# One planned order for four engines over the first phase of an attention and mixture-of-experts kernel

## The chip, the core and the metric

The kernel runs on one core of one Trainium2 chip. The metric is the device time in microseconds, the median of the runs. The engines are TensorE (PE in the rows; its weight loads are PEld), VectorE (DVE), ScalarE (ACT), GpSimd (POOL) and SyncE (SP), which issues most transfers.

## What is computed

```python
# q, k, v: (4, 8, 576, 64); window 64, causal
scores = q @ k.T / 8, masked to the last 64 positions
attn   = softmax(scores);  x = (attn @ v) as 2304 tokens x 512
# first MoE layer (dense): w_in 512x2048, w_out 2048x512
h = x @ w_in;  x = (h * sigmoid(1.702 * h)) @ w_out
# second: 8 experts, w1 512x1024, w2 1024x512, one expert a token
logits = x @ w_gate;  e = argmax(logits);  gate = softmax(logits)[e]
out = gate * (relu(x @ w1[e]) @ w2[e])
```

`w_in` and `w_out` come as 64-bit floating-point numbers, all else as 32-bit ones.

## The kernel before

**Chunks.** The 2304 tokens are nine chunks of 256 (`c`). Attention of a chunk is done in four pairs of heads (`p`), each in nine parts, the tuple `ATT`: `scores` (TensorE), `maxima` (VectorE), `exps` (ScalarE), `normalise` (two small VectorE operations and a 128x512 product, L239, on VectorE for chunks 0 and 1 and on GpSimd after), `probs_t` (TensorE transposes), `probs_out` (ScalarE, L253), `attend` (TensorE, L262), `x_hi` (ScalarE) and `x_lo` (VectorE). Every matmul operand is split into a high and a low part, and each product is done as three matmuls (L156 to L158, L163 to L166).

**Steps.** The first MoE takes 16 steps a chunk (`m`): `up_mm` (12 matmuls of 256 columns), `tanh` (ScalarE, L387), `act` (VectorE, L391), `g_hi` (ScalarE, L398), `g_lo` (VectorE, L404), `down` (6 matmuls of 512 columns). A step has a slot number; `down` of step m stands two slots behind its `up_mm`. Chunks 0 and 1 are interleaved, while the 16 weight blocks are loaded and converted (`CONV`: six parts on ScalarE and VectorE). The results stay in 8 `whi` and 8 `wlo` tiles of the pool `wp`, which has 8 of each; expert weights take the same tiles later.

**Routing.** After a chunk: two copies `y_out` (one ScalarE, one VectorE), 16 gate products `logits` (VectorE, L448; on TensorE for the last chunk), `route_a` and `route_b` (some 18 small VectorE operations, an exponential, two small matmuls) and two indirect scatters by GpSimd into `xbuf`, rows grouped by expert.

**The experts.** They run in order of their counts, with row capacities 384, 352, ... 256. `pick_first` names the first expert in the middle of the last chunk, `load_expert` and `prep_expert` bring its weights (`ws`) and split them (L151 ScalarE; L152, half on GpSimd and half on VectorE). The first expert's 256 rows known by then pass through seven of its steps (`SPLIT`) while the last chunk is routed. Then `pick_order`, the remaining rows, and the experts one after another follow.

**What sets the order.** TensorE's order is written out by hand all along (`manual_schedule`). Up to slot 31 (`MEND`) ScalarE, VectorE and GpSimd too follow a list, made by `plan()`: a small simulation with a price per part (`MODEL`: engine, us, PSUM banks taken and given back), which starts, whenever an engine is free, the first part by slot whose named dependencies are done, at most `AHEAD` slots early. Behind slot 31 the parts stand at slots chosen by hand (`at_slot`), and the compiler orders the three engines by its own model of costs. SyncE's queue is ordered by the compiler throughout.

Of the kernel before, what the change touches and what calls it, by code (L numbers as in the profile page):

```python
# [28 lines left out]
E = 8  # L29
# [23 lines left out]
def tile_model(  # L53
# [115 lines left out]
    sched = defaultdict(list)  # L169
# [197 lines left out]
    def w_lo(m, i):  # L367
        hi, lo = dst_t[m][i]
        eng = nc.gpsimd if (m, i) in LO_POOL else nc.vector
        eng.tensor_tensor(out=lo, in0=st_t[m][:, i], in1=hi.bitcast(F32), op=ALU.subtract)  # L370
# [84 lines left out]
    def y_transpose(c, b):  # L455
        t = ps.tile([P, KD, P], F32, tag="ps", name="yt")
        for k in range(KD):
            nc.tensor.transpose(t[:, k, :], r_t[c, b][:, k * P : k * P + P], ident)
        for z, eng in enumerate((nc.scalar, nc.vector)):
            yT = gp.tile([P, CH], F32, tag="th", name="yT", bufs=2)  # L460
            src = t[:, 2 * z : 2 * z + 2, :].rearrange("p k t -> p (k t)")
            if z == 0:
                nc.scalar.activation(out=yT, in_=src, func=AF.Copy)
            else:
                nc.vector.tensor_copy(out=yT, in_=src)
            yT_t[b, z] = yT

    def logits_pe(c, b):
# [8 lines left out]
        if b == 1:  # L477
            lg = sm.tile([P, 2, E], F32, tag="lgs", name="lgs")
            nc.vector.tensor_copy(out=lg, in_=lp.rearrange("p (b e) -> p b e", b=2))
            r_t[c] = lg  # L480

    def route_a(c):
# [13 lines left out]
        )  # L496
        nc.vector.tensor_tensor(out=lg, in0=lg, in1=mxb, op=ALU.subtract)
        nc.scalar.activation(out=lg, in_=lg, func=AF.Exp)
        r_t[c] = (ohb, lg)

    def route_b(c):
        (ohb, ex), ys0, ys1 = r_t[c], r_t[c, 0], r_t[c, 1]
        shp = [P, 2, E]
        rk = ps.tile([P, 512], F32, tag="ps", name="rk")
        rv = rk[:, 0 : 2 * E].rearrange("p (b e) -> p b e", b=2)
        nc.vector.tensor_tensor(out=cum[:, 1, :], in0=cum[:, 0, :], in1=ohb[:, 0, :], op=ALU.add)
        nc.tensor.matmul(out=rv, lhsT=tri, rhs=ohb, start=True, stop=False)
        nc.tensor.matmul(out=rv, lhsT=ones, rhs=cum, start=False, stop=True)
        sl = sm.tile(shp, F32, tag="sl", name="sl")
# [15 lines left out]
        for b, ys in enumerate((ys0, ys1)):  # L525
# [19 lines left out]
    def count_keys():  # L545
        rk = ps.tile([P, 512], F32, tag="ps", name="cn")
        nc.tensor.matmul(out=rk[0:1, 0:E], lhsT=ones[:, 0:1], rhs=cum[:, 0, :], start=True, stop=True)
        cnt = sm.tile([1, E], F32, tag="cnt", name="cnt")
# [7 lines left out]
    def pick_first():  # L556
        cnt, key = count_keys()
# [8 lines left out]
    def pick_order():  # L566
        cnt, key = count_keys()
# [20 lines left out]
        return cnt, rank  # L588
# [5 lines left out]
    xp2 = {}  # L594

# [37 lines left out]

    def load_rows(e, which_blocks=None):
# [14 lines left out]
    def rows_t(e, b):  # L649
# [6 lines left out]
        xg, ti, ga, eh, el = ex_t[e]  # L656
        n = blocks(e)[b][1]
        t = ps.tile([P, KD, P], F32, tag="ps", name="et")
        for k in range(KD):
# [3 lines left out]
        hv = eh[:, :, b * P : b * P + n]  # L663
        nc.scalar.activation(out=hv, in_=t[:, :, 0:n], func=AF.Copy)  # L664
        nc.vector.tensor_tensor(  # L665
            out=el[:, :, b * P : b * P + n], in0=t[:, :, 0:n], in1=hv.bitcast(F32), op=ALU.subtract
        )
        nc.vector.tensor_copy(out=ti[0:n, b : b + 1], in_=xg[0:n, b, DM + 1 : ROW])
        nc.vector.tensor_copy(out=ga[0:n, b : b + 1], in_=xg[0:n, b, DM : DM + 1])

    def e_up(e, m, c0=0, c1=None, skip=0):
# [7 lines left out]
        for k in range(KD):  # L679
# [5 lines left out]
            )  # L685
        if "o" in xp2:
# [516 lines left out]
```

## Time and profile before

| | us |
|---|---|
| median of 3 runs | 754.58 (754.38 to 758.11) |
| the profiled execution's own time | 757.56 |
| its span, first to last instruction | 755.8 |
| busy: TensorE | 720.1 |
| busy: VectorE | 474.4 |
| busy: ScalarE | 366.1 |
| busy: GpSimd | 90.9 |

The span is what the trace covers; the own time holds 1.8 us more around it. A busy time is the union of the recorded instructions of an engine. A matmul's recorded end includes its latency, so a busy TensorE need not issue without gaps; its starts tell that.

### The profile page before, as it was taken

The numbers are of one execution on the slowest core, as the hardware profiler recorded it, in microseconds if no ns is written. First come the engines' busy times: TensorE is split into PE (matmuls) and PEld (weight loads), VectorE is DVE, ScalarE is ACT, GpSimd is POOL, SyncE is SP. The second block draws the span as 40 slices with busy tenths as digits, with TensorE's granted clock in tenths as the row PEclk, the third lists the DMA queues.
The fourth block names the chain that finished last, engine by engine and source line by source line (L and its number), as shares of the span: only waits on it lengthen the run. The fifth ranks groups of instructions, "written<-read, shape, count | busy, mean of one in ns | idle before, by whom it ended". The sixth has DMA issues, their size and how long they took to land. (4 is left out here: it accounts for less than half of the span.)

```text
span 755.8 us, 14418 instructions
## 1 busy us (share of the span) xinstructions
PE 720.1 (95%) x5356; PEld 632.8 (84%) x5357; DVE 474.4 (63%) x1451; ACT 366.1 (48%) x911; POOL 90.9 (12%) x97
## 2 busy tenths in 40 slices
PE   4779999999999999999999999988999999999996
PEld 3569888788988898898889889867788888898995
DVE  5999876956774754945936737464487453768511
ACT  6899664443445344344535433252266533546410
POOL 2000011111211012021011110142100201101111
PEclk9899999999999999999999999999999999999999
DMA  9992279120223022112211000341498726797100
GB/s 342 385 380 112 87 273 309 39 88 15 102 75 100 4 74 102 53 50 75 74 38 66 1 29 1 103 145 59 139 306 293 275 84 232 253 325 244 74 26 26
DMA packets 45370, 103.16 MB, mean 136 GB/s; under 512 B 3951, under 2 KB 12143, under 8 KB 45040
## 3 DMA queue, kind: packets, MB, share of 16 engines
q1 hardware_dynamic: 42304, 92.74, 35.9%
q0 software_dynamic: 2992, 9.46, 3.3%
q8 instruction: 43, 0.70, 0.4%
q14 instruction: 31, 0.25, 0.1%
HBM read 86.41 MB, written 16.03 MB: 136 GB/s over the span
## 5 line engine op out<-in xcount | busy, mean ns | idle before, releaser
L156 PE MATMUL h<-xh,whi 128*128 128x256 f32 x576 | 165.1, 287 | 0.0
L158 PE MATMUL h<-xh,wlo 128*128 128x256 f32 x576 | 163.2, 283 | 0.1
L157 PE MATMUL h<-xl,whi 128*128 128x256 f32 x576 | 162.9, 283 | 0.0
L163 PE MATMUL y<-whi,gh 128*128 128x512 f32 x288 | 118.9, 413 | 5.3 <-ACT gh L398 5.3
L391 DVE SCALAR_TENSOR_TENSOR th<-th,h 128x256 f32<-128x256 f32 x144 | 60.1, 417 | 100.2 <-ACT th L387 99.4
L387 ACT ACTIVATE th<-h 128x256 f32<-128x256 f32 x144 | 54.7, 381 | 134.0 <-PE h L158 128.8
L156 PEld LDWEIGHTS h<-xh,whi 128*128 128x128 f32 x576 | 110.1, 191 | 6.2 <-issue 0.5
L164 PE MATMUL y<-wlo,gh 128*128 128x512 f32 x288 | 114.3, 397 | 0.0
L157 PEld LDWEIGHTS h<-xl,whi 128*128 128x128 f32 x576 | 110.0, 191 | 4.7
L158 PEld LDWEIGHTS h<-xh,wlo 128*128 128x128 f32 x576 | 109.9, 191 | 0.5 <-DVE wlo L370 0.5
L152 DVE TENSOR_TENSOR wlo<-ws,whi 128x1024 fp32r<-128x1024 f32 (+1 forms) x64 | 77.7, 1222 | 34.1 <-ACT whi L151 33.7
L398 ACT ACTIVATE gh<-th 128x256 fp32r<-128x256 f32 x144 | 60.0, 416 | 66.0 <-DVE th L391 64.8
L448 DVE CUSTOM_DVE_ANT_0 junk<-ys,wg 128x512 bf16<-128x512 f32 x128 | 89.1, 696 | 2.9 <-DMA wg<-in_w_gateT 1.5
L166 PE MATMUL y<-whi,gl 128*128 128x512 f32 x288 | 90.3, 395 | 0.6 <-DVE gl L404 0.4
L151 ACT ACTIVATE whi<-ws 128x1024 fp32r<-128x1024 f32 (+1 forms) x72 | 68.0, 960 | 40.9 <-DMA ws<-in_w 30.6
L156 PE MATMUL eh_ps<-eh,whi 128*128 128x256 f32 (+3 forms) x284 | 85.4, 301 | 0.7 <-ACT eh L664 0.7
L157 PE MATMUL eh_ps<-el,whi 128*128 128x256 f32 (+3 forms) x284 | 83.6, 294 | 0.3 <-DVE el L665 0.3
L158 PE MATMUL eh_ps<-eh,wlo 128*128 128x256 f32 (+3 forms) x284 | 83.5, 294 | 0.0
L404 DVE TENSOR_TENSOR gl<-th,gh 128x256 fp32r<-128x256 f32 x144 | 61.5, 427 | 25.2 <-ACT gh L398 21.6
L163 PEld LDWEIGHTS y<-whi,gh 128*128 128x128 f32 x288 | 54.7, 190 | 16.2 <-ACT gh L398 8.4
L239 POOL TENSOR_TENSOR pr<-pr,su 128x512 f32<-128x512 f32 x28 | 31.1, 1112 | 296.6 <-DVE su L237 190.4
L166 PEld LDWEIGHTS y<-whi,gl 128*128 128x128 f32 x288 | 53.9, 189 | 14.9 <-DVE gl L404 2.8
(135 smaller groups left out, 1177.3 us busy)
## 6 DMA issues: line engine op xcount, KB each, us to landing
ws<-in_w SPq DMA_DIRECT2D x64, 512.0 KB, 5.1
qkv<-in_qkv SPq DMA_DIRECT2D x36, 672.0 KB, 5.0
st<-in_w_in SPq DMA_DIRECT2D x16, 512.0 KB, 10.1
st<-in_w_out SPq DMA_DIRECT2D x16, 512.0 KB, 11.0
xbuf<-zt SPq DMA_DIRECT2D x8, 771.0 KB, 10.1
xg<-xbuf SPq DMA_DIRECT2D x17, 257.0 KB, 5.4
raw<-in_w SPq DMA_DIRECT2D x8, 512.0 KB, 7.2
wg<-in_w_gateT SPq DMA_DIRECT2D x2, 1024.0 KB, 15.7
```

Source lines behind the costliest of these rows:

```text
L151: nc.scalar.activation(out=hi, in_=raw, func=AF.Copy)
L152: lo_eng.tensor_tensor(out=lo, in0=raw, in1=hi.bitcast(F32), op=ALU.subtract)
L156: nc.tensor.matmul(out=o, lhsT=a[0], rhs=b[0], start=first, stop=False)
L157: nc.tensor.matmul(out=o, lhsT=a[0], rhs=b[1], start=False, stop=False)
L158: nc.tensor.matmul(out=o, lhsT=a[1], rhs=b[0], start=False, stop=last)
L163: nc.tensor.matmul(out=o, lhsT=a[0][:, s], rhs=b[0], start=first, stop=False)
L164: nc.tensor.matmul(out=o, lhsT=a[0][:, s], rhs=b[1], start=False, stop=False)
L166: nc.tensor.matmul(out=o, lhsT=a[1][:, s], rhs=b[0], start=False, stop=last)
L391: nc.vector.scalar_tensor_tensor(out=th, in0=th, scalar=1.0, in1=h_t.pop((c, m)), op0=ALU.add, op1=ALU.mult)
L398: nc.scalar.activation(out=gh, in_=th, func=AF.Copy)
L404: nc.vector.tensor_tensor(out=gl, in0=th, in1=gh.bitcast(F32), op=ALU.subtract)
L448: nc.vector.tensor_tensor_reduce(out=junk, in0=ys[:, 0:DM], in1=wg_t[e // 4][:, e % 4, :], scale=1.0, scalar=0.0, op0=ALU.mult, op1=ALU.ad ...
```

## The change

`normalise` does its product on VectorE in every chunk. `y_out` becomes `y_act` and `y_dve`; only the last chunk's second copy stays on VectorE. Expert 0's splits become `e_hi` (ScalarE) and `e_lo` (VectorE), GpSimd's half included. From chunk 3 on `attend_pair` issues the attention of two pairs and the next two pairs' scores as one part. Routing, gate, row, expert load and expert step functions are cut into parts by engine and get prices in `MODEL`; `plan()` then orders the whole first phase, the last chunk's routing, the loads of expert 0 and its first seven steps in one list. The manual order of ScalarE, VectorE and GpSimd is kept from the first slot until two steps behind that list. `pick_first` stands ahead of the last chunk, after chunk 6 is routed. Left out below: the same cutting of `y_transpose`, `logits_pe`, `rows_t`, `e_up` and `count_keys`, and the named dependencies of the routing and expert parts.

```diff
@@ -235,8 +234,7 @@
         pr, mx, su = unit_t[c, p]
         nc.vector.tensor_scalar_add(su, su, 1e-9)
         nc.vector.reciprocal(out=su, in_=su)
-        eng = nc.vector if c < 2 else nc.gpsimd
-        eng.tensor_tensor(
+        nc.vector.tensor_tensor(
             out=pr, in0=pr, in1=su.unsqueeze(2).to_broadcast([P, 4, P]), op=ALU.mult
...
@@ -417,13 +414,13 @@
     r_t = {}
-    def y_out(c, b):
-        ys = yp.tile([P, ROW], F32, tag="ys", name="ys")
-        if b == 0:
-            nc.scalar.activation(out=ys[:, 0:DM], in_=y_t[c][b], func=AF.Copy, scale=0.5)
-        else:
-            nc.vector.tensor_scalar_mul(ys[:, 0:DM], y_t[c][b], 0.5)
-        r_t[c, b] = ys
+    def y_act(c, b):
+        ys = r_t[c, b] = yp.tile([P, ROW], F32, tag="ys", name="ys")
+        nc.scalar.activation(out=ys[:, 0:DM], in_=y_t[c][b], func=AF.Copy, scale=0.5)
+
+    def y_dve(c, b):
+        ys = r_t[c, b] = yp.tile([P, ROW], F32, tag="ys", name="ys")
...
+    def ranks(c):
+        ohb = r_t[c][0]
...
+    def scatter(c):
+        su32 = r_t[c]
+        for b in range(2):
+            ys = r_t[c, b]
...
+        nc.scalar.activation(out=ew_t[e, j][0][:, 2 * z + h], in_=st_t[e, i][:, h], func=AF.Copy)
+
+    def e_lo(e, i, h):
+        j, z = divmod(i, 2)
+        hi, lo = [t[:, 2 * z + h] for t in ew_t[e, j]]
+        nc.vector.tensor_tensor(out=lo, in0=st_t[e, i][:, h], in1=hi.bitcast(F32), op=ALU.subtract)
     def load_rows(e, which_blocks=None):
...
     SLOTS = slot[NCH - 1, NM - 1] + 1
+    LAST = SLOTS - NM
+    END = NCH - 1
     DD = 2
...
-    DB = (0, 0.01, 0.02, 1, 3, 3.01, 4, 4.01, 4.02)
+    DB = (0, 0.01, 0.02, 0.03, 3, 3.01, 4, 4.01, 4.02)
...
-    RG = {0: (1, 0.6), 1: (5, 0.55), 2: (2, 0.5), NCH - 2: (1, 0.2), None: (1.5, 0.45)}
-    RL = (1, 2, 1, 2, 2, 3)
+    RG = {0: (1, 0.6), 1: (3, 0.55), 2: (2, 0.5), NCH - 2: (1, 0.35), None: (2, 0.45)}
...
-        return slot[c - 1, 0] + 8 * (p // 2) - (2 if c == 3 else 3)
-
+        return slot[c - 1, 0] + 8 * (p // 2) - 3
+
+    def attend_pair(c, q):
+        for p in (2 * q, 2 * q + 1):
+            attend(c, p)
+        if (c, q) != (END, 1):
+            scores_pair(*((c, 1) if q == 0 else (c + 1, 0)))
+
+    def scores_pair(c, q):
+        for p in (2 * q, 2 * q + 1):
+            scores(c, p)
...
+    def swap_pools():
+        at_cm.__exit__(None, None, None)
+        pools.append(tc.tile_pool(name="p2g", bufs=2, reuse_waits="tile"))
+        xp2["g"] = pools[0].__enter__()
+
+    def clear_rows():
+        with tc.issue_after(last_w[0].ins):
+            init_xbuf(yp.tile([P, ROW], F32, tag="ys", name="zt"))
...
-        normalise: ("DVE", 1.2, 0, 0), probs_t: ("PE", 0.5, 1, 0), probs_out: ("ACT", 0.6, 0, 0),
+        normalise: ("DVE", 0.95, 0, 0), probs_t: ("PE", 0.5, 1, 0), probs_out: ("ACT", 0.55, 0, 0),
         attend: ("PE", 0.7, 0, 0), x_hi: ("ACT", 0.35, 0, 0), x_lo: ("DVE", 0.4, 0, 1),
+        attend_pair: ("PE", 2.3, 2, 0), scores_pair: ("PE", 1.1, 2, 0),
...
+        y_act: ("ACT", 0.55, 0, 1), y_dve: ("DVE", 0.65, 0, 1), logits: ("DVE", 0.75, 0, 0),
+        route_a: ("DVE", 1.4, 0, 0), gate_exp: ("ACT", 0.22, 0, 0), ranks: ("PE", 0.1, 1, 0),
+        route_b: ("DVE", 1.7, 0, 1), scatter: ("POOL", 2.4, 0, 0),
+        y_transpose: ("PE", 0.45, 1, 0), yT_act: ("ACT", 0.4, 0, 0), yT_dve: ("DVE", 0.4, 0, 1),
+        logits_pe: ("PE", 1.0, 0, 0), lg_out: ("DVE", 0.2, 0, 1),
+        count: ("PE", 0.1, 1, 0), pick_first: ("DVE", 1.3, 0, 1), pick_order: ("DVE", 1.7, 0, 1),
+        load_expert: ("SP", 1.8, 0, 0), e_hi: ("ACT", 0.6, 0, 0), e_lo: ("DVE", 0.7, 0, 0),
+        first_rows: ("SP", 1.2, 0, 0), last_rows: ("SP", 0.6, 0, 0),
+        rows_t: ("PE", 0.5, 1, 0), rows_hi: ("ACT", 0.55, 0, 0), rows_lo: ("DVE", 0.9, 0, 1),
+        e_up: ("PE", 1.45, 1, 0), e_act: ("ACT", 0.4, 0, 0), e_rest: ("DVE", 0.4, 0, 1),
+        e_down: ("PE", 1.4, 0, 0),
+        load_gate: ("SP", 6.0, 0, 0), clear_rows: ("POOL", 1.0, 0, 0), swap_pools: ("NONE", 0, 0, 0),
     }
+    LAND = {"SP": 2.0, scatter: 2.9, load_expert: 3.5}
...
     def part(s, fn, *a, after=()):
-
-        if s < MEND:
-            parts[fn, a] = (s, [x for x in after if x is not None])
-        else:
-            at_slot(s, fn, *a, rank=1 if fn in ATT else 5)
+        parts[fn, a] = (s, [x for x in after if x is not None])
...
-                take += 2 * (k[0] is down and k[1][1] == 0)
-                if eng != "SP" and parts[k][0] > parts[left[0]][0] + AHEAD:
+                take += 2 * (k[0] in (down, e_down) and k[1][1] == 0)
+                if k[0] is logits_pe:
+                    take = 1 - k[1][1]
+                if k[0] is maxima and k[1][0] >= PAIR:
+                    give *= k[1][1] % 2
+                if k[0] is attend_pair and k[1] == (END, 1):
+                    cost, take = 1.1, 0
+                far = parts[k][0] - parts[left[0]][0]
+                if far > 3 * AHEAD:
+                    break
...
                     held = held or banks < take
                     continue
                 free[eng] = t + cost
...
+    part(att_slot(PAIR, 0), scores_pair, PAIR, 0, after=[(load_pair, (PAIR, p)) for p in range(2)])
+    for c in range(PAIR, NCH):
+        for q in range(2):
+            n = (c, 1) if q == 0 else (c + 1, 0)
+            after = [(probs_out, (c, p)) for p in (2 * q, 2 * q + 1)]
+            after += [(load_pair, (n[0], p)) for p in (2 * n[1], 2 * n[1] + 1) if n[0] < NCH]
+            part(att_slot(c, 2 * q) + 8, attend_pair, c, q, after=after)
...
-    for k, (fn, a) in enumerate(plan()):
-        at_slot(BEGIN + (MEND - 0.5 - BEGIN) * k / len(parts), fn, *a)
+
+    part(slot[0, NM - 1], load_gate, after=[(load_w, (NM - 1,))])
+    part(slot[0, NM - 1] - 3, clear_rows, after=[(load_w, (NM - 1,))])
...
+        y = [(y_act, (c, 0)), (y_dve if c == END else y_act, (c, 1))]
+        for b, (fn, a) in enumerate(y):
+            part(s + 0.01 * b, fn, *a, after=[
+                (down, (c, NM - 1)), (scatter, (c - 2 + b,)) if c else (clear_rows, ()),
+            ])
...
+    part(LAST - 1, swap_pools, after=[(x_lo, (END, p)) for p in range(4)])
+    part(LAST - 0.9, count, 0, after=[(route_b, (NCH - 3,))])
+    part(LAST - 0.8, pick_first, after=[(count, (0,))])
+    part(LAST + 9, first_rows, after=[(scatter, (NCH - 2,)), (pick_first, ()), (swap_pools, ())])
...
+    EW, ED = 5, 1.2
+    for i in range(8):
+        p = LAST + EW + ED * i
+        part(p - 3, load_expert, 0, i, after=[
+            (pick_first, ()), (swap_pools, ()), *[(e_lo, (0, i - 2, h)) for h in range(2)]
+        ])
+        for h in range(2):
+            part(p + 1 + 0.4 * h, e_hi, 0, i, h, after=[(load_expert, (0, i))])
+            part(p + 1.1 + 0.4 * h, e_lo, 0, i, h, after=[(e_hi, (0, i, h))])
...
+    part(SLOTS + 2, last_rows, after=[(scatter, (END,))])
+    part(SLOTS + 3, count, 1, after=[(route_b, (END,))])
+    part(SLOTS + 3.1, pick_order, after=[(count, (1,))])
...
+        staged = tc.manual_schedule(
+            engines={mybir.EngineType.Activation, mybir.EngineType.DVE, mybir.EngineType.Pool}
+        )
+        staged.__enter__()
+        for fn, a in plan():
+            fn(*a)
...
-        rows = load_rows(0, blocks(0)[2:])
-        cnt, rank = pick_order()
...
+            if i == 2:
+                staged.__exit__(None, None, None)
```

## Rows read from the trace of the kernel before

**Rows 1.** The page, busy us (share of the span) xinstructions, per engine.
```profile
PE 720.1 (95%) x5356; PEld 632.8 (84%) x5357; DVE 474.4 (63%) x1451; ACT 366.1 (48%) x911; POOL 90.9 (12%) x97
```

**Rows 2.** Busy time by stretch: length, busy us (x) per engine, PEclk, DMA share, GB/s.
```profile
139.30:142.70 3.40, 3.40 (x22) 2.72 (x19) 3.37 (x11) 2.23 (x11) 1.37 (x1) 0.50 0.46 164
135.70:142.70 7.00, 5.22 (x35) 4.32 (x34) 6.72 (x32) 5.04 (x21) 1.37 (x1) 0.76 0.23 81
...
25.10:57.80 32.70, 25.74 (x230) 21.23 (x227) 31.39 (x75) 31.49 (x75) 0.00 (x0) 0.98 1.06 383
57.80:126.60 68.80, 68.80 (x521) 61.07 (x519) 53.80 (x128) 50.07 (x115) 3.66 (x5) 1.00 0.55 191
142.70:456.70 314.00, 313.78 (x2575) 279.14 (x2574) 192.36 (x761) 136.35 (x429) 40.33 (x37) 1.00 0.17 57
456.70:507.90 51.20, 48.17 (x300) 42.13 (x299) 32.99 (x100) 19.84 (x47) 9.03 (x8) 1.00 0.27 83
507.90:537.30 29.40, 25.78 (x164) 22.04 (x163) 11.78 (x41) 7.41 (x19) 5.72 (x6) 1.00 0.23 64
```

**Rows 3.** Timeline of PE in chunk 4: start us, us, instruction; [idle before <-releaser].
```profile
257.81 0.28 PE L156 MATMUL h<-xh,whi 128*128 128x256 f32 x1
...
260.62 0.28 PE L156 MATMUL h<-xh,whi 128*128 128x256 f32 x1
...
262.05 0.40 PE L163 MATMUL y<-whi,gh 128*128 128x512 f32 x1
...
263.53 0.69 PE L262 MATMUL t<-pr,qkv 128*64 128x64 f32 x16
264.14 0.39 PE L156 MATMUL h<-xh,whi 128*128 128x256 f32 x1
...
265.77 0.69 PE L262 MATMUL t<-pr,qkv 128*64 128x64 f32 x16
```

**Rows 4.** Timeline of PE at the end of chunk 2's attention.
```profile
139.09 0.97 PE L262 MATMUL t<-pr,qkv 128*64 128x64 f32 x16 [1.78 <-ACT pr L253]
```

**Rows 5.** Waits in the last chunk: us in total, times, longest us.
```profile
ACT whi L151 <- DMA ws<-in_w: 7.1, 5, 2.5
```

**Rows 6.** Timeline of PE in the passage.
```profile
507.96 0.28 PE L156 MATMUL eh_ps<-eh,whi 128*128 128x256 f32 x1
...
514.18 0.66 PE L458 MATMUL yt<-ident,ys 128*128 128x128 f32 x4 [0.84 <-ACT ys L423]
...
537.39 0.44 PE L156 MATMUL eh_ps<-eh,whi 128*128 128x384 f32 x1 [0.69 <-ACT eh L664]
```

**Rows 7.** Groups by line and shape: busy us, mean ns | idle before <-releasers.
```profile
L404 DVE TENSOR_TENSOR gl<-th,gh 128x256 fp32r<-128x256 f32 x144 | 61.5, 427 | 25.2 <-ACT gh L398 21.6 <-PE y L166 2.9
L391 DVE SCALAR_TENSOR_TENSOR th<-th,h 128x256 f32<-128x256 f32 x144 | 60.1, 417 | 100.2 <-ACT th L387 99.4
L398 ACT ACTIVATE gh<-th 128x256 fp32r<-128x256 f32 x144 | 60.0, 416 | 66.0 <-DVE th L391 64.8
...
L387 ACT ACTIVATE th<-h 128x256 f32<-128x256 f32 x144 | 54.7, 381 | 134.0 <-PE h L158 128.8 <-PE rk L508 3.7 <-PE cn L547 1.5
...
L239 POOL TENSOR_TENSOR pr<-pr,su 128x512 f32<-128x512 f32 x28 | 31.1, 1112 | 296.6 <-DVE su L237 190.4 <-DVE ys L521 80.0 <-ACT pr L229 18.3
...
L370 DVE TENSOR_TENSOR wlo<-st,whi 128x512 fp32r<-128x512 f32 x32 | 21.0, 682 | 0.1
...
L152 DVE TENSOR_TENSOR wlo<-ws,whi 128x512 fp32r<-128x512 f32 x8 | 9.9, 1238 | 8.5 <-ACT whi L151 8.3
...
L239 DVE TENSOR_TENSOR pr<-pr,su 128x512 f32<-128x512 f32 x8 | 5.5, 691 | 0.3
...
L473 PE MATMUL lg<-wgk,yT 128*128 128x8 f32 x16 | 2.1, 253 | 0.1
```

**Rows 8.** Timeline of VectorE and of SyncE's queue, last routing and last row load.
```profile
525.02 0.17 DVE L515 CAST su<-s 128x2 uint32<-128x2 f32 x1
...
532.01 8.92 SPq L644 DMA_DIRECT2D xg<-xbuf  x4
```

More of the change, by code (lines that the diff above doesn't have):

```diff
@@ L587, in pick_order @@
         nc.vector.tensor_copy(out=order[:, 1:E], in_=key[:, 1:E])
-        return cnt, rank
+        cnt_t["order"] = (cnt, rank)
     ew_t = {}
@@ new lines, in tile_model @@
+        for b, (fn, a) in enumerate(y):
+            part(s + 0.01 * b, fn, *a, after=[
+                (down, (c, NM - 1)), (scatter, (c - 2 + b,)) if c else (clear_rows, ()),
+            ])
+        prior = [(scatter, (c - 1,))] if c else []
+        if c == END:
+            for b in range(2):
+                part(s + 0.02 + 0.1 * b, y_transpose, c, b, after=[y[b]])
+                part(s + 0.03 + 0.1 * b, yT_act, b, after=[(y_transpose, (c, b)), (up_mm, (c - 1, NM - 1))])
+                part(s + 0.04 + 0.1 * b, yT_dve, b, after=[(y_transpose, (c, b)), (yT_act, (0,))])
+                part(s + 0.05 + 0.1 * b, logits_pe, c, b, after=[(yT_act, (b,)), (yT_dve, (b,))])
+            part(s + 0.2, lg_out, c, after=[(logits_pe, (c, 1))])
+            ready, e = [(lg_out, (c,))], 0.21
+        else:
+            g = RG.get(c, RG[None])
+            for i in range(2 * E):
+                part(s + g[0] + g[1] * i, logits, c, i // E, (i % E,), after=[y[i // E], (load_gate, ())])
+            ready, e = [(logits, (c, i // E, (i % E,))) for i in range(2 * E)], g[0] + 16 * g[1]
@@ new lines, in tile_model @@
+        part(s + e, route_a, c, after=ready + [(route_b, (c - 1,))])
+        part(s + e + 0.01, gate_exp, c, after=[(route_a, (c,))])
+        part(s + e + 0.1, ranks, c, after=[(route_a, (c,))])
+        part(s + e + 0.2, route_b, c, after=[(ranks, (c,)), (gate_exp, (c,))])
+        part(s + e + 0.3, scatter, c, after=[(route_b, (c,)), (clear_rows, ())])
+    part(LAST - 1, swap_pools, after=[(x_lo, (END, p)) for p in range(4)])
+    part(LAST - 0.9, count, 0, after=[(route_b, (NCH - 3,))])
+    part(LAST - 0.8, pick_first, after=[(count, (0,))])
@@ new lines, in tile_model @@
+    last = [(END, NM - 1 - z) for z in range(3)]
+    for m in range(SPLIT):
+        i = SLOTS + m
+        up = [(e_lo, (0, 4 * (m // 4) + z, h)) for z in range(2) for h in range(2)]
+        dn = [(e_lo, (0, 4 * (m // 4) + 2 + z, h)) for z in range(2) for h in range(2)]
+        full = (0, m, 0, CH)
+        part(i, e_up, *full, after=up + [(rows_lo, (0, b)) for b in range(2)] + [
+            (e_up, (0, m - 1, 0, CH)) if m else (up_mm, last[0]),
+            (e_act, (0, m - 2)) if m > 1 else (tanh, last[1 - m]),
+        ])
+        part(i + 0.5, e_act, 0, m, after=[
+            (e_up, full), (e_down, (0, m - 3)) if m > 2 else (down, last[2 - m]),
+        ])
+        part(i + 0.55, e_rest, 0, m, after=[(e_act, (0, m))])
+        part(i + DD - 0.1, e_down, 0, m, after=dn + [
+            (e_rest, (0, m)), (e_down, (0, m - 1)) if m else (down, last[0]),
+        ])
@@ L1113, in tile_model @@
         xp2["o"] = p2o_cm.__enter__()
-        for b, _ in blocks(0)[2:]:
-            rows_t(0, b)
-        count_rows(cnt, rank)
-        with tc.issue_after(rows.ins):
+        count_rows(*cnt_t["order"])
+        with tc.issue_after(rows_in[-1].ins):
             load_rows(1)
@@ L1127, in tile_model @@
                 e_up(*steps[i])
+                e_act(*steps[i][0:2])
+                e_rest(*steps[i][0:2])
             if i > 1:
```

192 lines of the change are left out of this document (99 added, 93 removed).

## The prediction

> **What bounds the kernel now.** The span is 755.8 us and TensorE is busy for 720.1 us of it [rows 1], so at most 36 us stand idle, and the first question is where. The second view, busy time by stretch, was cut at the borders that the timeline shows: the head, the interleaved chunks 0 and 1, the end of chunk 2's attention, the steady chunks, the last chunk (number 8), the passage into the experts [rows 2]. In the steady stretch from 142.7 to 456.7 TensorE is busy for 313.78 of 314.00 us: nothing can be won there by filling waits. Waits stand in four places: the head (25.74 of 32.70 us, with VectorE at 31.39 and ScalarE at 31.49, so both are full), the seven microseconds from 135.7, the last chunk (48.17 of 51.20) and the passage (25.78 of 29.40).
>
> A busy share hides part of a loss, because a matmul's recorded end includes its latency. So the third view is the timeline of TensorE, read by starts. One step of the unit, an `up_mm` of 12 matmuls and a `down` of 6, repeats every 260.62 - 257.81 = 2.81 us, and a plain `up_mm` takes 262.05 - 260.62 = 1.43 us [rows 3]. Every figure below is a length by starts, less what the work in it takes at that pace.
>
> **What can be removed, place by place.**
>
> Split attention pairs (C). In the steady chunks a group reads: attention of one pair 0.61 us, an `up_mm`, attention of the next pair, then scores. The `up_mm` in between takes 265.77 - 264.14 = 1.63 us in place of 1.43 [rows 3]. The new `attend_pair` issues both attentions and the next two scores as one part, so that `up_mm` no longer stands between two changes of form: 0.20 us, and about 0.06 us of the second attention's own entry. The pattern stands 12 times (chunks 3 to 8, two halves each): 12 x 0.26 = 3.1 us.
>
> End of chunk 2's attention (B). Seven us from 135.7 [rows 2] hold one `up_mm` (1.43), one attention (0.61) and one `down` (2.81 - 1.43 = 1.38, about 1.5 beside an attention): 3.5 us of work, 3.5 us lost. TensorE waits 1.78 us for ScalarE's `probs_out` [rows 4]; then the granted clock is 0.50, the 1.2 GHz level, over the 3.4 us from 139.3 [rows 2], in which the same work takes about 1.7 us more. So here the wait is paid twice. In the passage, whose single waits are shorter, the clock stays at 1.00 [rows 2]. This place lies just behind slot 31, where the list of before ends.
>
> Last chunk (D). 51.2 us less 16 x 2.81 = 45.0 leave 6.2; two transposes of rows, a rank and a count are real work of about 1.4. Lost: 4.8 us. ScalarE stands 7.1 us in front of `whi<-ws`, waiting for expert 0's weights, with the next tile's tanh and copy queued behind it [rows 5].
>
> Passage (E). 537.39 - 507.96 = 29.4 us [rows 6] hold seven steps (19.7), the gate's 16 small matmuls (2.1 recorded [rows 7], about 1.9 by starts), eight transposes (0.9) and some 0.6 of rank, count and row transposes: 23.1. Lost: 6.3 us, of which 0.84 is the wait of the first four transposes, in TensorE's queue, for `ys` [rows 6]. The next step begins with another 0.69 us for `eh` [rows 6]: 7.0 together.
>
> In sum 3.1 + 3.5 + 4.8 + 7.0 = 18.4 us can go at most, the head aside.
>
> **The change, part by part.**
>
> The normalising product goes from GpSimd (28 of 1112 ns) to VectorE (691 ns, eight of them there already) [rows 7]: 28 x 0.69 = 19.3 us more for VectorE. Eight `y` copies leave VectorE for ScalarE; I count nothing for them. VectorE's share in the steady stretch is 192.36 of 314 [rows 2]; the six chunks there receive four products each, 16.6 us: 67%. On the path this costs nothing while VectorE's own queue does not delay a step. The cover is this: between an `up_mm`'s end and its `down` lie one `down` and one `up_mm`, 2.81 us, and the chain in that time is tanh, product, high and low part, 0.381 + 0.417 + 0.416 + 0.427 = 1.64 us and its handovers [rows 7]; about 1.0 us is spare. One product of 0.69 fits; what two blocks in a row cost is rival three.
>
> Expert 0's low halves: eight on GpSimd and eight on VectorE become 16 on VectorE. Beside GpSimd VectorE's took 1238 ns, where the same shape takes 682 ns in the MoE weights [rows 7]. So 16 x 0.68 = 10.9 us replace 9.9, and a low half is ready 0.56 us sooner. The bound from above, had the slow rate stayed, is 16 x 1.24 = 19.8, 9 us more on an engine with 18 us idle in that chunk [rows 2]: hidden either way.
>
> The same 0.56 us bears on the products: each that ran beside a two-input instruction of VectorE may have slowed it so, between none and all of 28, 0 to 15.7 us. VectorE's work then grows by 3.6 to 19.3 us; I take the upper end, since few of the products can have run so in a steady stretch where VectorE is busy 61%. The Trainium skill's page SBUF — State Buffer (Who interferes with whom) says that a VectorE instruction with two SBUF inputs and a GpSimd instruction that reads SBUF exclude each other for their whole length. The rows agree in direction; by the page the move could even relieve VectorE (31.1 us of GpSimd's products against 19.3). The sum would be the same, since VectorE is not on the path, but rival three, which I give 0.13, would fall to some 0.08.
>
> The single list replaces the compiler's order for VectorE, ScalarE and GpSimd behind slot 31, and also places TensorE's parts. How good such a list is can be read from its own stretch: from 57.8 to 126.6, most of it ordered by the old list, TensorE is busy 68.80 of 68.80 us with VectorE at 53.80 [rows 2]. The list's prices are near the rows, too (`w_lo` 0.67 to 0.682, `act` 0.37 to 0.417, 0.1 of handover added). It is right where its dependencies are complete, so I look for what it does not know.
>
> It does not know that expert 0's weights go into tiles of `wp`, of which all 8 `whi` and 8 `wlo` hold the first MoE's weights until the last chunk's steps 3 and 7. `e_hi` names only its load. The first load can follow `pick_first`, now ahead of the last chunk in place of its middle; by the list's own 1.3, 1.8 and 3.5 us the data are there about two steps into the chunk, while the tile is free after `up_mm` 3, 3.5 steps in. ScalarE is in order, so it would stand up to 1.5 steps, 4.2 us, with tanh behind it; the spare of 1.0 us leaves 3.2 us on TensorE, and the second and third tile add perhaps 1 us each. Bounds for what stays of D: nothing (the loads are now seven steps earlier, so none is late) and 5.2 us. I take 3.8, near the upper end, because the dependency is plainly absent. D gives 1.0 us.
>
> Place B lies behind the old list's end and within the new one, and its product no longer passes through GpSimd's queue. Bounds 0 and 3.5; I take 3.0, by the 68.80 of 68.80 next door.
>
> For E the question is the chain: `y`, transposes, gate, routing, scatter, last rows. From the first transposes (514.18 [rows 6]) to the copy of the slot numbers (525.02) pass 10.8 us, some 9 without waits; from there to the issue of the row load (532.01) 7.0 us [rows 8]; the next step starts 5.4 us later (537.39 [rows 6]), some 4 without its own waits. That is 20 us from the last `down`, and TensorE has six steps (16.9) and 3.4 of small work to do meanwhile: just covered. So most of E goes, not all: 5.0 of 7.0, between 2 and 7.0.
>
> C I take whole, 3.1, since the part is one unit whatever its place. The head was ordered by the same list with slightly other prices and both engines are full there: 0, with 3 us either way. Earlier `pick_order` and loads of expert 1 give nothing: I count no wait there that they shorten.
>
> New waits: `route_a` and `route_b` are now single blocks of 1.4 and 1.7 us by the list's prices, longer than the spare of 1.0, where the compiler's order could set steps between their instructions. By the old list's stretch, 68.80 of 68.80, such blocks cost nothing and the sum is 12.1; from above, sixteen of them at 0.6 us are 9.6 and the sum is 2.5. The list moves TensorE's parts around a block, so I take 0.1 us each, 1.6. The Trainium skill's page Perfetto Trace Analysis (Optimizing Scalar/DVE Operations) speaks against the blocks: engines that are not full can still leave gaps on others, and shorter instructions help there. No row shows it for routing, and by it the sum would be the lower of the two.
>
> Sum: 3.1 + 3.0 + 1.0 + 5.0 - 1.6 = 10.5 us. The profiled execution's own time is 757.56, 1.8 us around its span, so 747.1 for it; it lies 3.0 above the median 754.58, so the median goes to 744.
>
> **Rivals.**
>
> One: every wait goes. 18.4 us, 736. For it: the loads come earlier and the list's stretch shows no wait. Against: the dependency on the tiles of `wp` that the list lacks, and a passage just covered.
>
> Two: the gain is given back in chunk 8 and the passage. D grows to some 9 us as tiles block ScalarE, and the rows of the last chunk come after TensorE's cover, so that E gives 2: 3.1 + 3.0 - 4 + 2 - 1.6 = 2.5 us, 752. For it: the missing dependency. Against: a block in the queue also delays what it is measured against.
>
> Three, slower: VectorE's queue sets the pace. Each chunk from 2 to 7 gets four products and two routing blocks, 36 in all, placed whole. If a block comes in front of a step's product more than the spare allows, TensorE waits; from 0.30 us a block on, the 10.5 us are gone, and from 0.40 us on (14.3 us) the kernel is slower by over 0.5%. At 0.45 us: 760. For it: the spare of 1.0 us, which two blocks in a row exceed. Against it: the 68.80 of 68.80, and what leaving GpSimd gives back.
>
> **How the numbers follow.** Forecast (739 to 749) 0.50; rival one 0.15; rival two (749 to 757) 0.22; rival three 0.13. A measurement tells 0.5%, 3.8 us, from no change. Faster than 750.8: 0.50 + 0.15 + 0.05 = 0.70; within: 0.17; slower than 758.4: 0.13 (rival three in full). The range from 735 to 757 leaves out a little of rival one and most of rival three.
>
> **What would show it.** Right: no `up_mm` between two attentions; no clock of 0.50 near 139; the last chunk within 47 to 51 us; the passage below 26 us; VectorE about 15 us busier, GpSimd without its 31 us. Wrong: TensorE below 99% in the steady stretch, with waits for `th` or `gl` (rival three); ScalarE standing at `whi<-ws` for a TensorE release early in the last chunk (rival two); a head longer by more than 3 us.

## The result, and the profile after

The changed kernel takes 744.13 us (median of 6 runs, 743.17 to 748.78); the kernel before, run beside it, 756.52 (6 runs). The ratio is 0.985, with an interval from 0.982 to 0.988, and 12.4 us are gone. The forecast was 744, 10.5 us below a median of 754.58. The profiled execution took 745.15 us with a span of 743.5, 12.3 less than before.

The page's busy line, to be held against [rows 1]:

```profile
PE 716.6 (96%) x5356; PEld 633.7 (85%) x5357; DVE 485.8 (65%) x1479; ACT 368.9 (50%) x919; POOL 50.1 (7%) x61
```

GpSimd lost its 31 us of products and 11 of splits; VectorE, which took both over, is only 11.4 us busier. Busy time by stretch, cut at the places of [rows 2] (chunk 2's end, steady, last chunk, passage, and the 27 us behind it):

```profile
126.00:140.80 14.80, 14.80 (x146) 12.96 (x145) 13.77 (x55) 8.94 (x34) 0.00 (x0) 1.00 0.20 63
140.80:450.20 309.40, 309.33 (x2575) 277.67 (x2573) 205.45 (x792) 138.32 (x434) 14.41 (x14) 1.00 0.17 59
450.20:494.70 44.50, 43.59 (x287) 39.74 (x286) 34.70 (x103) 21.46 (x52) 2.17 (x2) 1.00 0.39 119
494.70:522.90 28.20, 27.51 (x177) 24.26 (x175) 10.43 (x42) 6.03 (x15) 2.20 (x3) 1.00 0.08 29
522.90:550.00 27.10, 24.98 (x162) 22.53 (x163) 18.34 (x50) 13.27 (x22) 2.93 (x2) 1.00 0.87 286
```

The stretch at half clock near 139 is gone, the steady stretch is as full as before and 4.6 us shorter, and the last chunk and the passage are nearly full. Busy shares do not say what was gained where. For that TensorE's starts were compared: the same instruction in both traces.

| TensorE's start of | before | after | gained so far |
|---|---|---|---|
| the ninth step (the head's end) | 59.25 | 60.81 | -1.6 |
| chunk 2's first step | 142.72 | 140.78 | 1.9 |
| chunk 8's first step | 456.72 | 450.16 | 6.6 |
| expert 0's first step | 507.96 | 494.71 | 13.3 |
| its first step with all rows | 537.39 | 522.87 | 14.5 |
| expert 1's second step | 560.06 | 547.40 | 12.7 |
| the last step | 742.98 | 730.35 | 12.6 |

So the head lost 1.6, the end of chunk 2's attention gave 3.5, the steady stretch 4.6, the last chunk 6.7, the passage 1.3, and 1.9 were given back behind it. Some work changed place. Two `down`s, 2.8 us, passed from the last chunk into the passage: like for like the last chunk gave 3.9 us and the passage 4.1, 8.0 together. Four transposes, 0.4 us, passed from the steady stretch to a place ahead of chunk 2's first step (20 stand there, 16 before): like for like the end of chunk 2's attention gave 3.9 and the steady stretch 4.2.

The pair, timeline of TensorE in chunk 4 (compare [rows 3]): both attentions in one run, the scores behind them, then the `up_mm`.

```profile
257.88 0.40 PE L163 MATMUL y<-whi,gh 128*128 128x512 f32 x1
...
259.36 1.15 PE L260 MATMUL t<-pr,qkv 128*64 128x64 f32 x32
260.44 1.10 PE L203 MATMUL s<-qkv 64*64 64x128 f32 x32
261.48 0.39 PE L156 MATMUL h<-xh,whi 128*128 128x256 f32 x1
```

TensorE's waits before, in the last chunk (first line) and in the passage (us in total, times, longest):

```profile
PE y L163 <- ACT gh L398: 2.5, 2, 1.5
...
PE yt L458 <- DVE ys L521: 0.9, 1, 0.9
PE yt L458 <- ACT ys L423: 0.8, 1, 0.8
PE y L163 <- ACT gh L398: 0.8, 1, 0.8
...
PE o L166 <- DVE gl L699: 0.5, 1, 0.5
```

The last chunk after. ScalarE stands for a tile of `wp` until `up_mm` 3 has read it, as the prediction feared, but TensorE loses 0.9 us by it, once:

```profile
ACT whi L660 <- PE h L157: 3.7, 1, 3.7
...
PE y L163 <- ACT gh L395: 0.9, 1, 0.9
```

Behind the passage is a wait that the sum did not have. ScalarE's timeline there: a split of expert 1's weights waits for its data, with two `g_hi` copies (L746) queued behind it.

```profile
537.75 0.26 ACT L746 ACTIVATE gh<-eh_ps 128x128 fp32r<-128x128 f32 x1
540.99 1.06 ACT L151 ACTIVATE whi<-ws 128x1024 fp32r<-128x1024 f32 x1 [2.98 <-DMA ws<-in_w]
...
543.67 0.42 ACT L746 ACTIVATE gh<-eh_ps 128x128 fp32r<-128x128 f32 x2
```

TensorE has used up its own work by then:

```profile
543.98 0.50 PE L163 MATMUL o<-whi,gh 128*128 128x512 f32 x1 [1.69 <-ACT gh L746]
```

The chain that ended last (start, us, what) shows what stands ahead of the data. The last rows are asked for at 518.75; then SyncE's queue reads seven expert numbers into registers, from 519.15 to 523.13, where the kernel before read one; only then come expert 1's rows and, at 525.02, its first weights:

```profile
518.75 0.35 SPq L677
519.15 0.28 SPq L628
519.75 0.27 SPq L628
...
522.57 0.26 SPq L628
...
523.34 0.35 SPq L677
...
525.02 5.66 DMA ws<-in_w
530.70 1.07 ACT whi L151
```

### The profile page after: what moved, and what is told of

Same layout as the page of the kernel before. It is cut to its first block, busy times and chain, and to the rows that moved or that the text cites. A ratio compares the mean times of both kernels' runs of the same rounds, so it can differ in the third digit from the quotient of the medians.

```text
span 743.5 us, 14379 instructions
## 1 busy us (share of the span) xinstructions
PE 716.6 (96%) x5356; PEld 633.7 (85%) x5357; DVE 485.8 (65%) x1479; ACT 368.9 (50%) x919; POOL 50.1 (7%) x61
## 4 chain that ended last, share of the span: by engine, by line
PE 79%; issue 9%; DMA 5%; DVE 3%; ACT 2%; POOL 1%; SPq 1%; POOLq 0%; ACTq 0%; DVEq 0%
PE y L163 9%; PE h L156 9%; PE h L158 9%; PE h L157 9%; PE y L164 9%; PE y L166 9%; PE eh_ps L156 3%; PE eh_ps L157 3%; PE eh_ps L158 3%; PE o L163 3%; PE o L164 3%; PE o L166 3%; PE t L260 3%; PE s L203 2%; DMA ws<-in_w 2%
## 5 line engine op out<-in xcount | busy, mean ns | idle before, releaser
L152 DVE TENSOR_TENSOR wlo<-ws,whi 128x1024 fp32r<-128x1024 f32 x56 | 67.8, 1219 | 23.2 <-ACT whi L151 23.1
L151 ACT ACTIVATE whi<-ws 128x1024 fp32r<-128x1024 f32 x56 | 58.6, 1057 | 37.5 <-DMA ws<-in_w 25.3
L228 ACT ACTIVATE pr<-pr,mx 128x128 f32<-128x128 f32 x144 | 55.9, 391 | 16.6 <-DVE mx L218 16.6
## 6 DMA issues: line engine op xcount, KB each, us to landing
xbuf<-zt SPq DMA_DIRECT2D x8, 771.0 KB, 12.6
```

The lines of the kernel that those rows point to most:

```text
L151: nc.scalar.activation(out=hi, in_=raw, func=AF.Copy)
L152: lo_eng.tensor_tensor(out=lo, in0=raw, in1=hi.bitcast(F32), op=ALU.subtract)
```

## The experiments

Ratios are to the kernel before, of the runs beside it, with their intervals. "Standing" is TensorE's time by starts above what the same matmuls usually take. In diffs and views `...` stands for lines left out.

**1. The products back on GpSimd, under the new list.**

```diff
-        nc.vector.tensor_tensor(
+        eng = nc.vector if c < 2 else nc.gpsimd
+        eng.tensor_tensor(
             out=pr, in0=pr, in1=su.unsqueeze(2).to_broadcast([P, 4, P]), op=ALU.mult
```

> The changed kernel, with the 28 products of the normalisation from chunk 2 on put back on GpSimd; the list of all engines stays as it is. Theory (the order made the gain, the engine of the product is free): the time stays within 1.5 us of the changed kernel's 744.1, a ratio to the kernel before of 0.983 to 0.987, and TensorE stays at 99% or more from chunk 2's first step to chunk 8's. Rival (GpSimd's slow product was behind the waits): the waits at the split pairs and at the end of chunk 2's attention come back, 12 times 0.26 and 3.5 us, and the time is 748 to 751. A third way: only the place with the shortest slack feels the longer product, chunk 2's last unit, some 0.6 to 2 us there.

743.69 us, ratio 0.984 [0.982, 0.986]: as fast as the changed kernel. The steady stretch is full, and chunk 2's first step starts at 139.83:

```profile
139.80:448.60 308.80, 308.80 (x2574) 277.44 (x2573) 198.75 (x770) 137.80 (x434) 36.90 (x36) 1.00 0.17 59
```

Under the list the product's engine is worth nothing. VectorE is 6.7 us less busy in this stretch than in the changed kernel, although 22 products, 15.2 us, left it: its `g_lo` takes 468 ns in the mean beside GpSimd's products, 422 without them, and the small 128x4 addition of `normalise` 291 against 171.

**2. The kernel before, with the pairs' attentions together.** In `DS` the second pair's slots change, and nothing else:

```diff
-        (0.015, 1, 1.5, 1.51, 5.005, 5.6, 8.005, 8.4, 8.41),
+        (0.01, 1, 1.5, 1.51, 5.005, 5.6, 8, 8.4, 8.41),
```

> The kernel before, with one edit: the second attention of each pair from chunk 3 on stands directly behind the first on TensorE, as in the changed kernel, and its scores too. Theory: the up_mm between the two attentions and its 0.26 us of standing go, 12 times, so 3.1 us, ratio 0.996, and the stretch from chunk 2's first step to chunk 8's shortens by about 3. Rival (the standing only moves to the step behind the pair): less than 0.5 us, ratio 0.999 to 1.001. If it is 4.6 us, the whole gain of the changed kernel in that stretch is this edit.

754.77 us, 0.9988 [0.9972, 1.0004], not told apart from no change. The trace shows more than the time: from chunk 4 on each pair gains 0.16 us, steadily; among chunk 2's steps about 1 us is lost, most of it in a new wait of 0.92 us for `g_hi`.

**3. The kernel before, with attentions and scores in one run.** As 2, and the scores of the next pair at slot 0 in place of 0.01 and 0.015, so that they stand ahead of the `up_mm`.

> The kernel before, with both attentions of a pair and the scores of the next pair in one run on TensorE from chunk 3 on, as the changed kernel has them; with the attentions alone together each pair gained 0.16 us, in the changed kernel 0.33. Theory (TensorE pays at each change from one kind of matrix product to another, and the changed kernel has two changes fewer in a pair): 0.33 a pair from chunk 4 on, 4 us or less in all, ratio 0.995 to 0.997. Rival (the second half came from the other engines' order): 0.16 a pair, as with the attentions alone, ratio 0.998 to 0.999.

752.79 us, 0.9962 [0.9947, 0.9977]. From chunk 3's ninth step to chunk 8's first, nine pairs give 2.39 us, 0.27 each. A whole chunk between 4 and 7 takes 52.33 us before, 52.02 in experiment 2, 51.81 here and 51.65 in the changed kernel, where a pair thus gives 0.34. Each change of the kind of product costs, and a group has five of them before (step, attention, `up_mm`, attention, scores, step), four in experiment 2, three here. The 0.16 us a chunk that are left belong to something else: once a chunk a step is 0.20 us longer here (an `up_mm` of 1.50 and a `down` of 1.52 us, at 321.80, in place of 1.43 and 1.39). As a chunk takes 51.65 us also with GpSimd's products (1) and with the list on TensorE alone (6), the pair's gain is TensorE's order. Ahead of that, chunk 2's steps and half of chunk 3's lose 2.4 us, so the stretch says more than the time.

**4. The kernel before, with chunk 2's products due earlier.**

```diff
-    DB = (0, 0.01, 0.02, 1, 3, 3.01, 4, 4.01, 4.02)
+    DB = (0, 0.01, 0.02, 0.03, 3, 3.01, 4, 4.01, 4.02)
```

> The kernel before, with one number: the products and what follows of chunk 2's attention are due 0.97 of a step earlier in its planner, as in the changed kernel. Theory: the wait of 1.78 us at 138.32 goes, and with it the stretch at half clock behind it, 3.5 us in all, ratio 0.995 to 0.996; everything behind it keeps its length. Rival (the wait is set by the length of ScalarE's queue and not by when the product is listed): no change, 0.999 to 1.001.

756.04 us, 0.9996 [0.9975, 1.0018]: the rival. TensorE's wait is there to the hundredth (it ends at 140.37; in the kernel before, at 139.09), and the half clock behind it too:

```profile
140.37 0.34 PE L262 MATMUL t<-pr,qkv 128*64 128x64 f32 x4 [1.78 <-ACT pr L253]
```

The number is only the place at which the part is written down; ScalarE's order there is the compiler's, which sets this `probs_out` behind four exponentials of the next unit.

**5. The kernel before, with the products on VectorE.** One line, `eng = nc.vector`.

> The kernel before, with the 28 products moved from GpSimd to VectorE and nothing else. Theory (the engine is worth nothing by itself): 755 to 757 against 755.9; VectorE is 28 times 0.69 us, 19 us, busier. Rival one (the shorter product also ends the wait at 138.32): 752 to 754. Rival two (VectorE's queue, in the compiler's order, gets in front of the steps): 758 or more.

752.95 us, 0.9969 [0.9951, 0.9988], a gain: rival one. ScalarE's timeline shows the compiler's order changed by the shorter product. `probs_out` now comes ahead of the exponentials:

```profile
135.14 0.58 ACT L253 ACTIVATE pr<-t 128x512 f32<-128x512 f32 x1
135.97 0.40 ACT L229 ACTIVATE pr<-pr,mx 128x128 f32<-128x128 f32 x1 [0.25 <-DVE mx L219]
```

The wait and the half clock go (3.7 us by starts); two new waits for `g_hi` in chunks 2 and 3, 1.2 us, take part of it back. So the 3.5 us at the end of chunk 2's attention come by either way: from VectorE without the list, or (experiment 1) from the list without VectorE.

**6. The list orders TensorE alone behind the head.** The other engines' written order ends at chunk 1's first step.

```diff
+        free = False
         for fn, a in plan():
+            if not free and fn is up_mm and a[0] == 1:
+                staged.__exit__(None, None, None)
+                free = True
             fn(*a)
...
-            if i == 2:
-                staged.__exit__(None, None, None)
```

> The changed kernel, in which the list orders the other engines only up to chunk 1's first step (where the kernel before stopped, too) and TensorE alone from there on; VectorE, ScalarE and GpSimd are ordered by the compiler behind it, TensorE's order is that of the changed kernel to the instruction. Theory (the gain of the split pairs is TensorE's order alone, the waits of chunk 8 and of the passage need the other engines' order): the steady stretch keeps its 4.6 us, the last chunk and the passage lose up to the 8 us that they gained, 748 to 752. First rival (TensorE's order is all): 744. Second rival (a TensorE list that counts on the other engines' order and does not get it waits everywhere): 756 or more.

748.37 us, 0.991 [0.988, 0.994]. Some 4 us come back, but not where the theory had them. The profiled run was its fastest, 746.54, so the trace holds 1.4 us of them. In it the steady stretch gains 5.0, the last chunk has no wait for `g_hi` at all, and expert 0's first step waits 1.3 us for its rows' halves. The largest loss is in the last part of the head, where the ninth step starts at 62.89 (59.85 to 60.81 with the whole list): TensorE's waits from 46 to 63 (for a weight split, `probs_out` and `g_hi`), with a stretch at half clock:

```profile
PE h L156 <- ACT whi L363: 1.9, 1, 1.9
PE t L260 <- ACT pr L251: 1.6, 1, 1.6
PE y L163 <- ACT gh L395: 1.1, 1, 1.1
```

**7. The tile rule that the list lacks.**

```diff
+            free = ((up_mm, (END, 3)), (down, (END, 3)), (up_mm, (END, 7)), (down, (END, 7)))[i // 2]
-            part(p + 1 + 0.4 * h, e_hi, 0, i, h, after=[(load_expert, (0, i))])
+            part(p + 1 + 0.4 * h, e_hi, 0, i, h, after=[(load_expert, (0, i)), free])
```

> The changed kernel, with the rule that its list lacks: a first split of expert 0 on ScalarE is listed only once the up_mm or down of chunk 8 that last reads its tile is done. Theory: ScalarE's stand of 3.7 us near 455 goes, and TensorE's stand of 0.91 us at 459.7 (1.07 us over the usual distance) with it: 743.1, the last chunk 43.5 us long. Rival (expert 0's weights then come late): the last chunk is as short, but the first expert steps wait for weights, and the time is 744 to 746. Second rival: the stand is too short to be worth anything by itself, 743.8 to 744.5.

744.24 us, 0.984 [0.982, 0.987]. Both halves of the theory's mechanism hold, the time does not: the last chunk is 43.39 us long in place of 44.55, and the first step with all rows starts at 520.47 in place of 522.87 (1.1 us of that it had already at chunk 8's first step). But expert 1's second step starts at 547.23, against 547.40. All of it is lost in between: 0.6 us in a wait for `g_lo` at 531.37, the rest at the stop behind the passage, now 1.9 us, and in a stretch at half clock behind it:

```profile
PE o L163 <- ACT gh L746: 1.9, 1, 1.9
```

**8. The register reads one by one.**

```diff
     def which(e):
...
+            if e > 1:
+                with tc.issue_after(last_x[0].ins):
+                    ev_t[e] = nc.values_load(order[0:1, e : e + 1], **args)
...
```

(`last_x` is the weight load issued last.)

> The changed kernel, with the numbers of experts 2 to 7 read into SyncE's registers only when each expert's first load is due; in the changed kernel seven such reads stand in a row from 519.15 to 523.13, in front of expert 1's rows and weights. Theory: expert 1's first weights are issued about 3.4 us earlier (near 521.6 on the changed kernel's time axis), the stand of 1.69 us of TensorE at 543.98 behind ScalarE's wait for weights goes, and the time is 742.3. Rival (the transfers are slowed by the scattered output that runs beside them, and start early enough anyway): the stand stays, 743.5 to 744.5.

741.19 us (740.83 to 742.25), 0.981 [0.979, 0.982], 2.9 us below the changed kernel. Expert 1's first weights are asked for at 520.03, the stop shrinks to 0.9 us, and expert 1's second step starts at 544.44, 3.0 earlier. 1.6 of that it had already at the first step with all rows (521.29), so this trace gives the reads 1.4: the stretch from there takes 23.15 us, against 24.53 in the changed kernel's profile, and 25.75 and 26.76 in experiments 1 and 7, where the clock fell at the stop. The reads are not the whole cause of the stop: counted from the first step with all rows, the kernel before asks for these weights later (at 541.19, 3.8 us behind) than the changed kernel (2.2 us behind) and has no such stop. There ScalarE, in the compiler's order, never has more than one `g_hi` between two splits; in the changed kernel two stand behind the split that waits.

**9. Both mends (7 and 8).**

> The changed kernel with both mends: the tile rule for expert 0's first splits and the register reads one by one. Alone the tile rule shortened the last chunk by 1.2 us and lost it behind the passage, where expert 1's weights were late; alone the reads took 2.9 us off. Theory (the weights after the passage are the floor against which the first gain was lost): with the floor lowered part of the 1.2 us comes through, 740.0 to 740.8. Rival (the floor has only moved and is met again at once): 741.2, nothing beyond the reads alone.

740.24 us (739.68 to 740.53), 0.980 [0.977, 0.982]: within the theory's range. The ratio does not tell it from experiment 8's 0.981; the trace does, with 93.60 us from chunk 8's first step to expert 1's second against 95.71. The wait for `eh` at the passage's end stays; behind it none is left, and expert 1's second step starts at 542.58. It beats both kernels.

**10. The first expert chosen late.**

```diff
-    part(LAST - 0.9, count, 0, after=[(route_b, (NCH - 3,))])
+    part(LAST - 0.9, count, 0, after=[(route_b, (NCH - 3,)), (up_mm, (END, 8))])
```

> The changed kernel, with the choice of the first expert held back until chunk 8's step 8 is done, so that its loads and splits fall into the last third of the chunk, where the kernel before had them; the list plans the rest around that. Theory (the last chunk's waits went because the splits now spread over its whole length): part of the 3.8 us of waits comes back at the end of the chunk, and expert 0's first steps may wait for their weights, 747 to 750. Rival (what the list knows of all engines is enough, wherever the splits stand): 744 to 745.

740.51 us, 0.979 [0.976, 0.982]: the theory fell, and the rival was too modest. With the splits bunched in the last third, where the kernel before had them, TensorE's only waits from chunk 8 to expert 1 are two for rows:

```profile
PE et L693 <- DMA xg<-xbuf: 1.1, 2, 1.0
```

The stand at the tile is gone, because the loads now come after the tiles are free, and the stop behind the passage as well. There the same split waits 2.92 us for its weights (539.40), but one more `g_hi` stands ahead of it in ScalarE's queue, at 536.21. The register reads were not mended here, so the stop goes without earlier weights too, and the place of that `g_hi` is the difference that the trace shows.

**11. Late choice, and the list on TensorE alone from chunk 8 on.** Edits 10 and 6 together, the latter with `a[0] == END`.

> The changed kernel with two edits at once: the first expert chosen late (after chunk 8's step 8), and the list ordering TensorE alone from chunk 8's first step on, the other engines left to the compiler there. With the late choice alone the last chunk had no wait for ScalarE, and with TensorE's list alone neither. Theory (each of the two, early splits or a listed ScalarE, is enough to keep the splits out of the way of the steps, and with both gone ScalarE is late again): TensorE waits for g_hi near the end of chunk 8 for 2 to 4 us, and the time is 3 to 5 us above the late choice alone (740.5), 743 to 746. Rival (the order on TensorE itself made the gain, with the splits off GpSimd): the last chunk stays free of waits, 740 to 742.

743.0 us, 0.983 [0.980, 0.986]. The time lies in the theory's range, for another reason: the last chunk is free of waits for ScalarE, as the rival had it. The waits of TensorE from 448.6 to 494.4, and from there to 545:

```profile
PE et L693 <- DMA xg<-xbuf: 0.3, 1, 0.3
```

```profile
PE o L163 <- ACT gh L746: 1.5, 1, 1.5
PE yt L455 <- ACT ys L419: 0.6, 1, 0.6
PE yt L455 <- DVE ys L534: 0.3, 1, 0.3
```

The 2.5 us against experiment 10 are the copies ahead of the transposes and the stop behind the passage.

**12. The kernel before, with chunk 8's transposes one step later.** `RL = (1, 2, 1, 2, 2, 3)` becomes `(2, 3, 2, 3, 3, 4)`.

> The kernel before, with the transposes and logits of chunk 8 one step later among the first expert steps, where the changed kernel has them. Theory (TensorE's waits of 0.84 and 0.89 us at 513.9 and 515.5 for the copies of the chunk's output go, because a step stands in front of them): 1.7 us in the passage, ratio 0.9975. Rival (the routing ends a step later, so the scattered rows, the last rows and expert 1's weights come 2.8 us later and TensorE waits for those): 755.5 to 757, no gain or a loss.

755.12 us, 0.9993 [0.9975, 1.0012]: inconclusive in time, since the 1.7 us lie just inside the interval. In the trace the passage takes 27.98 us against 29.44 (28.60 to 29.35 in experiments 2 to 5, where its order is the old one). Both waits at the transposes are gone, a wait for rows is new, and the others stay:

```profile
PE y L163 <- ACT gh L398: 0.8, 1, 0.8
...
PE et L660 <- DMA xg<-xbuf: 0.4, 1, 0.4
PE o L166 <- DVE gl L699: 0.3, 1, 0.3
```

## Why the prediction was right, and where its sum was not

The time was met within a few tenths, and that closeness is luck: 10.5 us were forecast from 754.58, and 12.4 went from 756.52. The mechanism, waits and changes of kind that an order removes, was right, and the terms cancelled. Like for like the pairs gave 4.2 (3.1 forecast), the end of chunk 2's attention 3.9 (3.0), last chunk and passage 8.0 (6.0), and the 1.6 taken off for new waits did not come; against this stand 1.9 given back behind the passage and 1.6 in the head, neither in the sum.

**Pairs and new waits** (3.1 less 1.6 forecast, 4.6 measured in the steady stretch, 4.2 like for like). The pair was undersized, at 0.26 us against 0.34. The 0.20 for the `up_mm` was right; what was too small is the second attention's own entry, "about 0.06 us": two attentions take 1.08 us in one run (259.36 to 260.44) and 0.62 each apart, so it is 0.16, the gain of experiment 2. Twelve pairs at 0.34 are 4.1 us. The 1.6 us for the routing blocks were not there: no wait at one, in a stretch 309.33 of 309.40 us full. (The seven experiments with the list's order on TensorE take 308.5 to 309.0 us there.) Rival three, VectorE's blocks pacing the step, fell with that.

**End of chunk 2's attention** (3.0 forecast, 3.5 measured, 3.9 like for like). Nearly right in size, if a little above the bound of 3.5, and paid twice as said: wait and half clock went together. The reason given, that the place now lies within the list, is sufficient by experiment 1, but it is not the only one: leaving GpSimd's product does it as well (5). The moved number in `DB`, alone, does nothing (4).

**Last chunk and passage** (1.0 and 5.0 forecast; like for like 3.9 and 4.1 by starts). Passage: four waits went, and the one for `eh`, 0.69 us, stayed. The prediction's 7.0 to be won counts that wait twice, since 537.39 is a start behind it and the 29.4 us hold it already. Last chunk: this is the term that was mis-sized. ScalarE's stand for a tile came as worked out, 3.7 us early in the chunk (up to 4.2 forecast), but "leaves 3.2 us on TensorE", with a further us for each of the next two tiles, was wrong: TensorE lost 1.07 us, once. The list had set `up_mm` 2 and 3 in a row there (455.80 to 458.68), 1.4 us of work that the prediction's cover, one `down` and one `up_mm`, does not have.

The 2.5 us of waits near the chunk's end went, too. Early splits are not needed for that (10), a written order of ScalarE is not needed (6), and neither is (11). What these runs share is TensorE's own order, in which an `up_mm` is three or four steps ahead of its `down` late in the chunk (in 10 and 11 three, in places), where the kernel before kept two throughout, and the splits on VectorE, at 0.69 us each in place of 1.24 beside GpSimd. No run here separates the two. The traces lean to the first: in experiment 6 (first line) ScalarE stood 4.05 us for weights, with the `up_mm`s four ahead, and TensorE did not wait; before (second line), two ahead, a stand of 2.51 us was followed by TensorE's wait of 1.5.

```profile
492.06 0.63 ACT L660 ACTIVATE whi<-ws 128x512 fp32r<-128x512 f32 x1 [4.05 <-DMA ws<-in_w]
...
491.83 1.15 ACT L151 ACTIVATE whi<-ws 128x512 fp32r<-128x512 f32 x2 [2.51 <-DMA ws<-in_w]
```

Two signs were not met as worded: the last chunk took 44.5 us (47 to 51 said) and the passage 28.2 (below 26 said), because two `down`s, 2.8 us, moved from one to the other. And a sign of rival two, ScalarE standing at a split for TensorE, came without rival two's cost.

**Head** (0 within 3). The profile shows 1.6 us lost, but that is where the half clock fell: the ninth step starts between 58.90 and 60.74 in the six profiles with the head of before (mean 59.96), and between 59.85 and 60.81 in the seven with the whole list's head (mean 60.27). Counting the falls of the clock between 30 and 60 us: without one it starts at 58.90 and 59.25, with one between 59.85 and 60.74 under either order, with two, in the changed kernel's profile, at 60.81. Whether the list makes a fall likelier (seven profiles of seven, against four of six) is open.

**Behind the passage** (nothing forecast, 1.9 given back). "Earlier `pick_order` and loads of expert 1 give nothing" looked at what they would shorten, not at what comes late when everything in front moves up 14 us and SyncE's queue has seven reads in a row. Experiments 7 to 9 show that this was the next bound: a gain of 1.2 us ahead of it was worth nothing until the queue was shortened. The queue is not all that makes the stop: ScalarE's order behind the list bears on it too (8 and 10), and no run changes that order alone.

**VectorE** ("about 15 us busier" as a sign, 19.3 in the working, 11.4 measured). Two things make the difference. The eight `y` copies, for which nothing was counted, took 5.5 us with them (nine took 6.1 before). And the products alone, in experiment 5, make VectorE 13.0 us busier, between the bounds of 3.6 and 19.3; the upper end was the wrong choice. The Trainium skill's page SBUF — State Buffer (Who interferes with whom) says that a two-input VectorE instruction and a GpSimd instruction that reads SBUF shut each other out; experiment 1 agrees, with `g_lo` at 468 against 422 ns. By that page the rise would have been the smaller one. As VectorE is not on the path, nothing hung on it.

## What to carry to other kernels

When waits are taken out over a long stretch, look for the first thing behind it that does not move up with it, and at the queue that feeds it: a gain ahead of that bound counts for nothing until the bound moves. Read a compiler's order from the trace before crediting an engine: moving work from one engine to another can gain by changing the order on a third. On a full TensorE, count the changes between kinds of product: here a `down` ahead of an attention takes 1.48 us in place of 1.39, and an `up_mm` between two attentions 1.63 in place of 1.43. Order alone removes them.

## What the runs showed of the hardware

Seven register reads from memory by SyncE took 3.98 us in a row, 0.57 each, ahead of every transfer queued behind them.

The granted clock fell to 0.50, the 1.2 GHz level, behind single stops of TensorE in stretches otherwise full: for `probs_out` near 140, 1.75 to 1.78 us, in the kernel before and in experiments 2, 4 and 12, and behind the passage, 1.8 and 1.9 us, in experiments 1 and 7 (from 542.67 and 543.15). Each time it was back after 3.4 us. Behind the stops of 1.69, 1.4, 0.9 and 1.5 us at the same place in the changed kernel and in experiments 6, 8 and 11 it stayed at 1.00. In the crowded head it fell once or twice more at places that differ between profiles of the same order (32.39 in experiment 8, 44.81 in 7, 45.07 in 9), as in the changed kernel:

```profile
32.10:35.50 3.40, 3.40 (x24) 2.25 (x18) 3.33 (x12) 3.40 (x13) 0.00 (x0) 0.50 1.04 374
45.80:49.10 3.30, 3.30 (x12) 2.81 (x11) 3.23 (x9) 3.30 (x10) 0.00 (x0) 0.50 1.06 379
```
